# End states of a chunked mLSTM: VectorE copies the products' sums, GpSimd decays and adds the middle state

## The chip, the cores and the metric

The kernel runs on one core of a Trainium2 chip. The time is the device time of one execution in microseconds (us); the number given for a kernel is the median of its runs, 461.69 us for the kernel before (three runs). Five engines work side by side, each on its own queue in order: TensorE (PE in the profile, its weight loads PEld), VectorE (DVE), ScalarE (ACT), GpSimd (POOL) and SyncE (SP, which here only issues DMAs). They wait for one another through semaphores.

## The reference

An mLSTM cell with exponential gates runs over 4 batches x 8 heads, 768 steps, head size 40. Its output goes, token by token, through a two-layer network with a quick GELU (320 to 2048 to 320).

```python
for t in range(S):
    m_new = np.maximum(f_gate[:, :, t] + m, i_gate[:, :, t])
    f_stab = np.exp(f_gate[:, :, t] + m - m_new)
    i_stab = np.exp(i_gate[:, :, t] - m_new)
    C = f_stab * C + i_stab * outer(v_t, k_t)        # per head, 40 x 40
    n = f_stab * n + i_stab * k_t                    # per head, 40
    y_t = sigmoid(o_t) * (C @ q_t) / max(|n . q_t|, 1)
...
h = x @ w_in
g = h * (1.0 / (1.0 + np.exp(-1.702 * h)))
return g @ w_out
```

## The kernel before

**Windows.** The 768 steps are cut into six windows of 128 (w = 0 to 5). A window's attention is done in chunked form. For w of 1 and more, a window has two halves of 64 steps, and C and n together (40 x 41 per head) are a state that is known at three places: at the window's start (`state[w % 2]`), between the halves (`state_mid`) and at its end (`state[1 - w % 2]`). Sixteen pairs of heads lie in the free direction in two sets c = 0, 1 of eight pairs, so that one set of states is a 128 x 328 tile (8 x 41 columns).

**How a new state is made.** `carry` (L598) multiplies keys by gated values (`vw`, made by `scale` on GpSimd, L592) on TensorE. The sums for the middle state land in the PSUM tile `pair[0]`, those for the end state in `pair[1]`. The middle state is the start state times a decay plus the first sum: GpSimd multiplies (`decay` with x = 0, L583) ahead of the products, VectorE adds the sum (L616). The end state is the middle state times a second decay plus the second sum: VectorE multiplies (`decay` with x = 1, L583), and VectorE adds (L616). Both are done for c = 0, then for c = 1. Window 0 has one half and ScalarE copies its sums; window 5 needs no end state. So the two VectorE instructions per set run in windows 1 to 4.

**Who reads and who waits.** `values` (L515) of the same window multiplies queries by the start and the middle state. The end state is read first by `decay` of the next window. `pair` is also the PSUM tile of `scores` (L463) and of `values` (L507, L515): the scores of set c are written to `pair[c]`, which must have been read by VectorE before. VectorE multiplies the scores by the gate weights `wt` (L466). These weights are exponentials from ScalarE (L439, 16 per set) that GpSimd masks (`affine_select`, L443, two per set). After the second group of products, VectorE makes the outputs `u` (L521, L522, then L473 to L482). `u` and `vw` share a pool of two buffers (tag "u").

**Order.** There is no scheduler that reorders; every engine's queue has the order of the program text. The attention of window w + 1 is dealt out in pieces (`attention`, L926) between the blocks of the down projection of window w: after blocks of four f-tiles (`down`, L798) while w is 0, after the seven products of a Strassen-like scheme for each token half (`down_fast`, L852, with VectorE's additions L857 and `last_sums` L837) for w of 1 and more. Behind the attention pieces VectorE's queue holds, in window 1, four transposes of queries (L398) and the conversion of two pieces of the output weights (L256, L257, L259, L265), then the scores' product L466; in windows 2 to 4 two `last_sums` (L837), two additions (L857), then L466. GpSimd's queue holds `scale`, `decay`, four masks, and then, in window 1, a wait for the weights (`mark`, L596) and the weight sums (L811); in windows 2 to 4 nothing until the next up projection (`up_fast`, L729, L708, with GpSimd's L789).

Of the kernel before, what the change touches and what calls it, by code (L numbers as in the profile page):

```python
# [12 lines left out]
OP = mybir.AluOpType  # L13
# [13 lines left out]
def kernel(  # L27
# [14 lines left out]
    BH = B * H  # L42
# [5 lines left out]
    D1 = D + 1  # L48
# [6 lines left out]
    NJ = PH // 2  # L55
# [8 lines left out]
    op = ctx.enter_context(tc.tile_pool(name="op", bufs=2))  # L64
# [5 lines left out]
    V, A, G, T = nc.vector, nc.scalar, nc.gpsimd, nc.tensor  # L70
# [27 lines left out]
    def k_cols(w, t, h):  # L98

        return k_of(w)[t, h, 0:D] if w < 2 else k_st[t, h * D:h * D + D]  # L100
# [121 lines left out]
    state = [const.tile([128, BH // 2, D1], FP, name=f"state{i}") for i in range(2)]  # L222
    state_mid = const.tile([128, BH // 2, D1], FP, name="state_mid")

    m_at, ends = {0: m0}, {}
    cols, stacked, m_row, raw = {}, {}, {}, {}
    kT, qT, ys, xT, gs, o_ps, sums, vw, x_row = {}, {}, {}, {}, {}, {}, {}, {}, {}
# [105 lines left out]
    def slot(i, x):  # L333

        return slice((x ^ i) * HL, (x ^ i) * HL + HL)
# [239 lines left out]
            for n, k in ((0, slice(0, 2)), (1, slice(2, 3))):  # L575
                V.transpose(out=x[:, :, k], in_=x_square(c, n)[:, 4 * b:4 * b + 4].rearrange("p n (d c) -> p n c d", d=32))

    def decay(w, c, x, engine=G):

        js = slice(c * NJ, (c + 1) * NJ)  # L580
        d = cols[w][:, 3 * BH + x * BH // 2:3 * BH + (x + 1) * BH // 2][:, js]
        old, dst = ((state[w % 2], state_mid), (state_mid, state[1 - w % 2]))[x]
        engine.tensor_tensor(out=dst[:, js], in0=old[:, js], in1=d.unsqueeze(2).to_broadcast([128, NJ, D1]),  # L583
                             op=OP.mult)

    def scale(w, c, part=0, parts=1):
        n = PH // parts
# [10 lines left out]
    def carry(w, cs):  # L598
        n = 2 if 0 < w < NW - 1 else 1
        for c in cs:  # L600
            for j in range(NJ):
                for i in range(2):
                    for x in range(n):
                        t = slot(i, x) if w else slice(0, L)
                        T.matmul(pair[x][i * 64:i * 64 + D, c, j * D1:(j + 1) * D1],  # L605
                                 k_cols(w, t, c * PH + 2 * j + i), vw[w, c][t, 2 * j + i, :], start=True, stop=True)
        for x, dst in enumerate((state_mid, state[1 - w % 2])[:n]):
            for c in cs:
                js = slice(c * NJ, (c + 1) * NJ)
                new = pair[x][:, c, 0:NJ * D1].rearrange("r (j d) -> r j d", d=D1)  # L610
                if w == 0:
                    A.copy(out=state[1][:, js], in_=new)
                    continue
                if x:
                    decay(w, c, x, V)
                V.tensor_tensor(out=dst[:, js], in0=new, in1=dst[:, js], op=OP.add)  # L616


    def up(w, j, between):
# [305 lines left out]

    def attention(w):  # L926
        at = (0, 1, 3, 3, 5, 6, 8, 8, 9, 12, 14) if w == 1 else (0, 0, 1, 3, 1, 4, 5, 6, 6, 10, 11)
        calls = [[(columns, w), (scale, w, 0), (scale, w, 1), (decay, w, 0, 0), (decay, w, 1, 0)],
                 [(weights, w, 0)], [(weights, w, 1)], [(carry, w, (0, 1))], [(open_gates, w)],
                 [(scores, w, 0), (scores, w, 1)], [(values, w, 0)], [(seam_out, w, 0), (seam_in, w, 0)],  # L930
                 [(values, w, 1), (seam_out, w, 1), (seam_in, w, 1)], [(seam_turn, w, 0)], [(seam_turn, w, 1)]]
        side = {}
        for i, c in zip(at, calls):
            side.setdefault(i, []).extend(c)
        return side

    for w in range(NW):
        more = w + 1 < NW
        if w == 0:
            for j in range(NF // 2):  # L940
                if j % 2 == 0:
                    ahead, behind = converted[j // 2]
                    run([(convert, p) for p in ahead] + [(fetch, p) for p in fetched.get(j // 2, ())])
                    up(w, j, lambda: run([(columns_turn, 1) if p is None else (convert, p) for p in behind]))
                if j == 6:
                    load(1, "o")
                if j == 1:
                    wait_for(w_in_sb[:, 1, 512:1024])
                    scale(0, 1)
                    load(1, "v")  # L950
                if j < B and j % 2:
                    carry(0, (j // 2,))
                if j == 3:
                    masks()
                    gates(1)
                    columns_in(1)
                if j == 4:
                    spread(1)
                    load_squares(1, "q")
                if j >= B:  # L960
                    transposes(1, j - B)
        else:
# [23 lines left out]
            gelu_fast(w, NF // 2 - 1)  # L986
            hidden_sums(w, (2, 3), V)
        side = attention(w + 1) if more else {}
        if w == 0:

# [53 lines left out]
```

## Time and profile before

| | |
|---|---|
| runs | 461.58, 461.69, 464.37 us; median 461.69 |
| profiled execution | 463.3 us, of which the span of the trace is 461.6 us |
| TensorE busy | 452.8 us of the span, granted clock 1.00 |
| VectorE busy | 350.9 us |
| ScalarE busy | 186.0 us |
| GpSimd busy | 162.7 us, 155 instructions |
| VectorE, decay of the middle state (L583) | 8 instructions, 6.1 us |
| VectorE, adding the end sums (L616, `state`) | 8 instructions, 4.0 us |
| GpSimd, decay of the start state (L583) | 10 instructions, 9.3 us |
| GpSimd, masks (L443) | 20 instructions, 23.4 us |

A row of the timeline reads: start in us, length in us (of a run of equal instructions, from the first start to the last end), engine, line, operation, output and inputs, shapes, count, and in brackets the idle time of the engine before it with the event that ended it. A row of the waits reads: who waited for whom, us in total, times, longest. The chip's own wait instructions do not count as busy.

### The profile page before, as it was taken

Reading aid. Unit: us, or ns where it says so; the run is one execution under the profiler, and the core shown is the slowest. Engines: PE = TensorE matmul, PEld = TensorE weight load, DVE = VectorE, ACT = ScalarE, POOL = GpSimd, SP = SyncE. Lnnn points to the kernel's source line nnn. Section 1 sums busy time; section 2 is a strip of 40 time slices with the busy share of each in tenths; the row PEclk is TensorE's granted clock in tenths of the full one; section 3 lists DMA queues with packets and bytes.
Section 4 is the critical chain, followed back from the end, with each engine's and each line's share of the span. In section 5 each row is a group of like instructions: output and inputs, shape, how many; then the busy total and the mean of one; then the engine's idle time right before and its main releaser. Section 6 shows DMA issues by size and latency. Waiting matters only on the chain.

```text
span 461.6 us, 12375 instructions
## 1 busy us (share of the span) xinstructions
PE 452.8 (98%) x5071; PEld 386.5 (84%) x5071; DVE 350.9 (76%) x738; ACT 186.0 (40%) x433; POOL 162.7 (35%) x155
## 2 busy tenths in 40 slices
PE   8999999999999999999899999999999999999996
PEld 6777877775779999779899779999888999787996
DVE  6788998899988876889786888787788767554622
ACT  5686779100546600546700354900264810164100
POOL 5101318130677500266700167610157710146200
PEclk9999999999999999999999999999999999999999
DMA  8999999038969044959224979315989505000000
GB/s 165 186 289 195 251 234 221 5 67 186 179 138 122 3 102 115 193 79 174 36 61 109 195 117 165 50 37 122 176 130 156 76 18 141 28 1 1 1 28 30
DMA packets 135561, 52.87 MB, mean 115 GB/s; under 512 B 101984, under 2 KB 131632, under 8 KB 135504
## 3 DMA queue, kind: packets, MB, share of 16 engines
q1 hardware_dynamic: 127136, 50.27, 56.0%
q10 hardware_dynamic: 8048, 1.66, 1.8%
q8 instruction: 40, 0.66, 0.7%
q0 software_dynamic: 320, 0.15, 0.2%
q14 instruction: 17, 0.14, 0.1%
HBM read 44.52 MB, written 7.54 MB: 113 GB/s over the span
## 4 chain that ended last, share of the span: by engine, by line
PE 75%; DVE 11%; ACT 4%; SPq 4%; DMA 3%; issue 2%; DVEq 0%; ACTq 0%
PE p_out L852 30%; PE p_h L729 16%; PE p_a L729 6%; PE p_h L631 5%; PE p_h L708 4%; PE p_a L708 3%; SPq L120 2%; PE p_a L507 2%; DMA st_row<-f_run 2%; PE p_a L515 2%; PE p_a L463 2%; PE p_a L605 2%; ACT wt L439 2%; PE p_h L640 1%; PE p_a L390 1%
## 5 line engine op out<-in xcount | busy, mean ns | idle before, releaser
L789 POOL TENSOR_TENSOR g<-g,parts 128x512 f32<-128x512 f32 x30 | 38.2, 1274 | 184.7 <-ACT g L746 175.9
L768 ACT COPY parts<-p_h 128x256 f32<-128x256 f32 x40 | 14.9, 372 | 164.6 <-PE p_h L729 159.5
L852 PE MATMUL p_out<-w_out_sb,g 128*128 128x160 f32 x480 | 68.9, 300 | 0.0
L852 PEld LDWEIGHTS p_out<-w_out_sb,g 128*128 128x128 f32 x480 | 66.4, 190 | 0.5
L697 ACT ACTIVATE g<-g 128x512 f32<-128x512 f32 x80 | 47.7, 629 | 23.8 <-DVE g L783 18.8
L857 DVE TENSOR_TENSOR o_sb<-o_sb,p_out 128x160 f32<-128x160 f32 x70 | 21.4, 317 | 43.6 <-PE p_out L852 43.0
L852 PE MATMUL p_out<-t_sb,s 128*128 128x160 f32 x320 | 47.1, 300 | 0.0
L729 PE MATMUL p_h<-xT,w_in_sb 128*128 128x256 f32 x160 | 45.4, 386 | 0.0
L852 PEld LDWEIGHTS p_out<-t_sb,s 128*128 128x128 f32 x320 | 44.4, 190 | 0.2
L729 PE MATMUL p_h<-t_x,s_in 128*128 128x256 f32 x160 | 41.2, 380 | 0.2 <-DVE t_x L684 0.2
L439 ACT ACTIVATE wt<-wt,cols 128x64 f32<-128x64 f32 x160 | 38.8, 333 | 0.1
L729 PEld LDWEIGHTS p_h<-xT,w_in_sb 128*128 128x128 f32 x160 | 29.4, 190 | 9.8 <-issue 6.3
L798 PE MATMUL p_out<-w_out_sb,g 128*128 128x320 f32 x128 | 35.7, 436 | 0.0
L729 PEld LDWEIGHTS p_h<-t_x,s_in 128*128 128x128 f32 x160 | 30.2, 190 | 4.8 <-DVE t_x L684 0.6
L798 PEld LDWEIGHTS p_out<-w_out_sb,g 128*128 128x128 f32 x128 | 23.9, 190 | 9.6
L769 DVE TENSOR_TENSOR t_x<-p_h,parts 128x256 f32<-128x256 f32 x40 | 17.0, 425 | 16.8 <-ACT g L697 8.7
L631 PE MATMUL p_h<-xT,w_in_sb 128*128 128x256 f32 x128 | 29.6, 384 | 0.0
L631 PEld LDWEIGHTS p_h<-xT,w_in_sb 128*128 128x128 f32 x128 | 23.6, 190 | 5.3 <-issue 2.4
L820 POOL TENSOR_TENSOR g<-g 128x512 f32<-128x512 f32 x20 | 25.5, 1276 | 0.0
L443 POOL TENSOR_SCALAR_AFFINE_SELECT wt<-wt 64x1024 f32<-64x1024 f32 x20 | 23.4, 1170 | 5.4 <-ACT wt L439 4.7
L852 PE MATMUL p_out<-w_out_sb,s 128*128 128x160 f32 x160 | 23.8, 302 | 0.0
L852 PE MATMUL p_out<-t_sb,g 128*128 128x160 f32 x160 | 23.8, 302 | 0.0
(221 smaller groups left out, 892.4 us busy)
## 6 DMA issues: line engine op xcount, KB each, us to landing
q_sq<-in_q_dram SPq DMA_DIRECT2D x20, 320.0 KB, 10.2
wt<-m_row SPq DMA_DIRECT2D x20, 256.0 KB, 5.6
k_sq<-in_k_dram SPq DMA_DIRECT2D x16, 320.0 KB, 6.3
out_dram<-o_sb SPq DMA_DIRECT2D x24, 160.0 KB, 1.9
eo<-in_o_gate_dram SPq DMA_DIRECT2D x5, 640.0 KB, 8.5
bits<-in_moe_w_in_dram SPq DMA_DIRECT2D x6, 512.0 KB, 11.4
q_sq<-x_row SPq DMA_DIRECT2D x10, 256.0 KB, 2.9
v_st<-in_v_dram SPq DMA_DIRECT2D x14, 160.0 KB, 5.9
```

The source lines that it names most:

```text
L439: A.activation(out=x[:, h, :], in_=x[:, h, :], func=AF.Exp, scale=-1.0, bias=cols[w][:, c * PH + h:c * PH + h + 1])
L443: G.affine_select(out=r, in_=r, compare_op=OP.is_ge, fill=0.0, base=0, pattern=[[0, PH], [1, HL]], channel_multiplier=-1)
L631: T.matmul(ph[j][i][:, t], w_in_sb[:, c, f * 128:(f + 1) * 128], x[:, c, t], start=(first and c == 0 and n == 0), stop=(not first and c == ...
L697: A.activation(out=gs[w, j][:, i, :], in_=gs[w, j][:, i, :], func=AF.Gelu_apprx_sigmoid)
L708: T.matmul(row[:, t], w_in_x[r, j, :], xT[w][r, 2].rearrange("p b t -> p (b t)")[:, t], start=(start and h == 0), stop=(not start and h == ...
L729: T.matmul(out, a, x[n], start=start, stop=stop)
L769: V.tensor_tensor(out=u2, in0=p56[:, right], in1=y[:, left], op=OP.add)
L789: G.tensor_tensor(out=g0, in0=g0, in1=u, op=OP.add)
L798: T.matmul(po, gs[w, f // 2][:, f % 2, b * L:(b + 1) * L], w_out_sb[:, f, :], start=(f == 0), stop=(f == NF - 1))
L820: G.tensor_tensor(out=a10, in0=a00, in1=a10, op=OP.subtract)
L852: T.matmul(po, a(f), b[:, f, :], start=(f == 0), stop=(f == NH - 1))
L857: V.tensor_tensor(out=dst, in0=x, in1=po, op=OP.add)
```

## The change

VectorE no longer multiplies the middle state by its decay and no longer adds for the end state: in windows 1 to 4 it copies the second sum from PSUM into the end state's tile. Two new GpSimd instructions per set, at the end of `carry` and so behind the four masks in GpSimd's queue, multiply the middle state by its decay into the first 328 columns of the set's `vw` buffer, which the products have been read from by then, and add that to the end state's tile. `decay` keeps only its first form. The numbers of instructions per window: VectorE 6 before and 4 after, GpSimd 4 more.

```diff
-    def decay(w, c, x, engine=G):
+    def decay(w, c):
         js = slice(c * NJ, (c + 1) * NJ)
-        d = cols[w][:, 3 * BH + x * BH // 2:3 * BH + (x + 1) * BH // 2][:, js]
-        old, dst = ((state[w % 2], state_mid), (state_mid, state[1 - w % 2]))[x]
-        engine.tensor_tensor(out=dst[:, js], in0=old[:, js], in1=d.unsqueeze(2).to_broadcast([128, NJ, D1]),
-                             op=OP.mult)
+        d = cols[w][:, 3 * BH + c * NJ:3 * BH + (c + 1) * NJ]
+        G.tensor_tensor(out=state_mid[:, js], in0=state[w % 2][:, js], in1=d.unsqueeze(2).to_broadcast([128, NJ, D1]),
+                        op=OP.mult)
...
                 if w == 0:
                     A.copy(out=state[1][:, js], in_=new)
-                    continue
-                if x:
-                    decay(w, c, x, V)
-                V.tensor_tensor(out=dst[:, js], in0=new, in1=dst[:, js], op=OP.add)
+                elif x == 0:
+                    V.tensor_tensor(out=dst[:, js], in0=new, in1=dst[:, js], op=OP.add)
+                else:
+                    V.tensor_copy(out=dst[:, js], in_=new)
+        if n == 2:
+            for c in cs:
+                js, old = slice(c * NJ, (c + 1) * NJ), vw[w, c][:, 0:NJ, :]
+                d = cols[w][:, 3 * BH + BH // 2 + c * NJ:3 * BH + BH // 2 + (c + 1) * NJ]
+                G.tensor_tensor(out=old, in0=state_mid[:, js], in1=d.unsqueeze(2).to_broadcast([128, NJ, D1]), op=OP.mult)
+                G.tensor_tensor(out=state[1 - w % 2][:, js], in0=state[1 - w % 2][:, js], in1=old, op=OP.add)
...
-        calls = [[(columns, w), (scale, w, 0), (scale, w, 1), (decay, w, 0, 0), (decay, w, 1, 0)],
+        calls = [[(columns, w), (scale, w, 0), (scale, w, 1), (decay, w, 0), (decay, w, 1)],
```

## The prediction

> **What bounds the kernel now.** I read the page's busy table first, then TensorE's waits, then the timeline of each engine around the four places where the end state is made.
>
> ```profile
> PE 452.8 (98%) x5071; PEld 386.5 (84%) x5071; DVE 350.9 (76%) x738; ACT 186.0 (40%) x433; POOL 162.7 (35%) x155
> ```
>
> TensorE is busy for 452.8 of 461.6 us. Whatever VectorE saves is worth only what it takes out of TensorE's 8.8 us of idle time. So the question is which part of that idle time is a wait for VectorE behind the edited instructions. TensorE's waits (us in total, times, longest):
>
> ```profile
> PE p_h L729 <- DVE xT L576: 0.9, 1, 0.9
> PE p_a L507 <- DVE wt L466: 0.7, 3, 0.3
> PE p_a L463 <- DVE state L616: 0.6, 1, 0.6
> PE p_h L729 <- DVE t_x L684: 0.2, 1, 0.2
> ```
>
> These are 2.4 us, all on VectorE. The other named waits in that list belong to the start of the kernel, to a key load (0.6) and to issue. TensorE's timeline places them:
>
> ```profile
> 89.73 0.97 PE L507 MATMUL p_a<-v_st,wt 64*64 64x41 f32 x41 [0.26 <-DVE wt L466]
> 111.23 0.70 PE L729 MATMUL p_h<-xT,s_in 128*128 128x256 f32 x2 [0.87 <-DVE xT L576]
> 112.09 1.16 PE L729 MATMUL p_h<-t_x,s_in 128*128 128x256 f32 x4 [0.16 <-DVE t_x L684]
> ...
> 160.20 1.24 PE L507 MATMUL p_a<-v_st,wt 64*64 64x41 f32 x64 [0.20 <-DVE wt L466]
> ...
> 229.07 1.16 PE L463 MATMUL p_a<-qT,kT 40*64 40x64 f32 x64 [0.62 <-DVE state L616]
> ...
> 303.28 1.24 PE L507 MATMUL p_a<-v_st,wt 64*64 64x41 f32 x64 [0.20 <-DVE wt L466]
> ```
>
> So window 1 holds 1.29 us (0.26 + 0.87 + 0.16), window 2 0.20, window 3 0.62 and window 4 0.20. Now VectorE in window 1, and GpSimd beside it:
>
> ```profile
> 77.12 0.55 DVE L583 TENSOR_TENSOR state<-state_mid,cols 128x328 f32<-128x328 f32 x1
> 77.77 0.50 DVE L616 TENSOR_TENSOR state<-p_a,state 128x328 f32<-128x328 f32 x1
> 78.19 1.18 DVE L583 TENSOR_TENSOR state<-state_mid,cols 128x328 f32<-128x328 f32 x1
> 79.40 0.50 DVE L616 TENSOR_TENSOR state<-p_a,state 128x328 f32<-128x328 f32 x1
> 79.82 2.04 DVE L398 STREAM_TRANSPOSE qT<-q_sq 128x512 f32<-128x512 f32 x2
> ```
>
> ```profile
> 77.88 2.49 POOL L443 TENSOR_SCALAR_AFFINE_SELECT wt<-wt 64x1024 f32<-64x1024 f32 x2 [0.56 <-ACT wt L439]
> ```
>
> The multiply (L583) has two SBUF inputs and takes 0.49 at best; beside GpSimd's masks it takes 1.18 here and 1.24 in window 3. The addition (L616), with one input in PSUM, takes 0.49 to 0.50 in all eight cases, masks or not. The same holding-up is seen a little earlier:
>
> ```profile
> 70.19 1.39 DVE L257 TENSOR_SCALAR w_out_sb<-w_out_sb 128x512 uint32<-128x512 uint32 x1
> 71.62 1.66 DVE L259 SCALAR_TENSOR_TENSOR w_out_sb<-t_sb,w_out_sb 128x512 uint32<-128x512 uint32 x1
> 73.42 1.01 DVE L265 CUSTOM_DVE_ANT_0 w_out_sb<-t_sb,w_out_sb 128x1024 uint16<-128x1024 uint16 x1
> ```
>
> Beside GpSimd's `vw` multiplies (69.75 to 72.7) the conversion's 0.43 and 0.69 become 1.39 and 1.66: such an instruction waits for the end of the GpSimd instruction that it meets.
>
> **The change part by part.**
>
> *VectorE, removed: 8 multiplies*, 6.1 us in all (mean 761 ns). *Changed: 8 additions into copies from PSUM.* No row shows a 128x328 copy; the nearest are the copies from PSUM of 128x160 at 0.318 (an addition of that size: 0.317) and of 128x320 at 0.48. I take 0.49, equal to the addition, and nothing for the difference; the ends are 0.48 and 0.50. Being a PSUM read, I expect no hold-up by the masks.
>
> *GpSimd, added: 16 instructions*, 4 in each of windows 1 to 4. The multiply has a row of its own shape: L583 on GpSimd, 0.73 undisturbed, 0.95 on average, 1.18 at most. The addition has none; between 128x512 at 1.274 and 128x1280 at 2.904 the slope is 2.12 ns per element, and for 328 elements I work out an estimate of 0.88. A pair is 1.61, a window's four are 3.2, 13 us in all on an engine that is 35% busy. They lie behind the masks, so the masks are not later. Behind them in the queue: in window 1 the wait for the weights, which started at 90.16 and would now be reached at about 83.5; in windows 2 to 4 nothing before the next up projection some 20 us later. I cost them at nothing on GpSimd's own queue.
>
> *The new waits.* (a) GpSimd's additions wait for VectorE's copies, done before the last mask. (b) VectorE's L521 writes `u` into the buffer that GpSimd's first pair uses, and now waits for that pair. Window 2: masks end at 158.27, plus 1.61 gives 159.9; L521 starts at 162.54, or 162.3 if TensorE gains 0.2. Windows 3 and 4: about 231.6 against 234.1, and 303.0 against 305.4. Each has 2.4 us to spare; the second pair ends some 5 us before the second L521. Nothing is added.
>
> *The Trainium skill* (GPSIMD Engine Reference, "Engine selection") advises against exactly this move: two-input elementwise work belongs on VectorE, GpSimd being about twice as slow. The rows here say 0.73 against 0.49, 1.5 times; by the page's factor a pair would be an estimate of 2.0 us, still inside the 2.4 us, and the sum would not move.
>
> *Window 1.* VectorE's L398 starts at 79.82; without the two multiplies, and at the spacing of 0.41 between L616's, it starts at 77.12 + 2 x 0.41 = 77.95: 1.87 us earlier. But the four transposes (3.83 us) end then at 81.78, and the conversion's L256, L257 and L259 meet the new GpSimd instructions, which run from about 80.25 to 83.5. Before, GpSimd was idle from 80.38 on. L256 meets the first addition's last 0.1; L257 waits for the second multiply, about 0.6; L259 for the second addition, about 0.7. That takes 1.3 from 1.87, and about 0.6 is left. The ends: no hold-up, 1.87; all three held for a whole addition, 3 x 0.88 = 2.6, so 0.8 later than before. I take 0.6, as it follows the pattern of the three rows shown last. Behind that, VectorE is occupied without a gap from 92.09 to the token sums at 113 (L473 at 93.84 takes 2.39 instead of 0.17 until GpSimd's L811 ends, but L811 starts after L466 and moves with it), so TensorE gains what VectorE gains, up to its 1.29 us of waits: 0.6.
>
> *The rule behind this* is in the Trainium skill (SBUF — State Buffer, "Who interferes with whom"): GpSimd shares a pair of ports with VectorE as an exclusive lock for a whole instruction, against one-input VectorE work in a two-port mode and against two SBUF inputs, but not against at most one SBUF input. L616's steady 0.49 and L257's 1.39 agree. Without the lock window 1 would give 1.29 instead of 0.6, and the sum 2.3 instead of 1.6.
>
> *Window 2.* Additions at 153.35, copies from 154.17, `last_sums` (L837) from 155.0 instead of 156.28, then ahead of the masks that start at 155.86; L857 and L466 are ready by about 156.7 instead of 158.93. TensorE's L507 then follows its predecessor at 160.0: 0.20. *Window 4* is the same in every row: 0.20. *Window 3.* Copies end at 226.7, before TensorE has done the first set of scores (227.29 + 1.16), so the 0.62 goes; L837 is then held by masks until about 228.6, L466 starts at about 229.1 and ends its first half at 230.3, before L507 is due at 231.9. Next late there is nothing. 0.62.
>
> *Sum:* 0.6 + 0.20 + 0.62 + 0.20 = 1.6 us. Against the profiled execution's own 463.3 (span 461.6 and 1.7 around it) this gives 461.7. That execution is 1.6 above the median of the runs; from the median 461.69 the forecast is **460.1 us**.
>
> **The rivals.**
>
> *A: the hold-up eats window 1's gain, or more.* For it: the three rows above. Against it: only three instructions overlap. Windows 2 to 4 keep 1.0; window 1 gives 0 to -0.8: 460.7 to 461.5.
>
> *B: the gain does not last.* TensorE's carry products in window 3 waited 0.57 for a key load (223.57). If that chain of transfers did not move with TensorE, the 0.8 of windows 1 and 2 would reappear there: 460.9. Against it: the chain starts at VectorE's scan at 187.56, which follows TensorE.
>
> *C: slower, by VectorE's wait for the `u` buffer.* Place: L521 in windows 2 to 4. It begins to delay VectorE once a GpSimd pair takes 4.0 us instead of 1.61, TensorE (whose L507 at 164.77 has 0.5 to spare behind L522) from 4.5, and it makes the kernel slower than before from 5.0, since three windows then lose the 1.6 gained. At 6 us per pair: 3 x 1.5 - 1.6 = 2.9 slower, 464.6. For it: GpSimd's L583 stretches from 0.73 to 1.18 beside VectorE. Against it: VectorE runs only PSUM readers (L857, L466) there, and two at 1.3 make 2.6.
>
> **How the numbers follow.** The forecast has 0.58, its own range 459.4 (all 2.3 us of waits gone) to 461.0. A has 0.20, B 0.12, C 0.10. The range reaches down to 458.8 (the 2.3, and the key load's 0.57 gone too) and up to 462.3 (A's 461.5 and half of the 1.6 by which executions of the same kernel differ). A change of under 1%, 4.6 us, is about what a measurement of this kernel cannot tell from none. Faster by more would need twice the VectorE waits there are: 0.02. Slower by more needs C with pairs of over 6.5 us: 0.04. Within: 0.94.
>
> **What would show it.** Right: no L583 on VectorE, copies from PSUM at 0.49; L398 in window 1 some 1.9 us closer to L616; L257 and L259 there at about twice their 0.43 and 0.69; GpSimd pairs of about 1.6 us behind the masks; TensorE's waits for L616 gone, for L466 gone, for L576 at 0.3 to 0.7. Wrong: a wait of L521 for GpSimd; copies that stretch beside the masks; TensorE busy for the same share of an unchanged span.

## The result and the profile after

| | before | after |
|---|---|---|
| runs of this comparison | 8, 461.58 to 464.37 us | 8, 459.02 to 460.00 us |
| median | 462.17 us | **459.68 us** |
| ratio | | **0.9944**, 95% interval 0.9933 to 0.9954 |
| profiled execution, its span | 463.3, 461.6 us | 459.97, 458.3 us |

The kernel became faster by 0.56%, which is 2.6 us (2.1 to 3.1) of 462.2. The forecast was 460.1 us and a gain of 1.6. The time lies in the range, but the gain is an us larger than the terms of the sum.

The busy table after, the same line as at the head of the prediction:

```profile
PE 452.1 (99%) x5071; PEld 386.4 (84%) x5071; DVE 341.4 (75%) x730; ACT 185.5 (40%) x433; POOL 175.3 (38%) x171
```

VectorE lost 9.5 us and 8 instructions, GpSimd gained 12.6 us and 16. Of the 3.3 us by which the profiled span became shorter, 0.7 are busy time of TensorE (452.8 to 452.1) and the other 2.6 are idle time. TensorE's waits for VectorE behind the edited instructions were four groups with 2.4 us in all; after, two are left, with 0.6:

```profile
PE p_h L734 <- DVE xT L576: 0.4, 1, 0.4
PE p_h L734 <- DVE t_x L689: 0.2, 1, 0.2
```

The waits of the second products (L507) for `wt` and of the scores (L463) for the state are gone. The new instructions, from the views of their three lines (count: shortest/median/longest ns, first and last start, shapes):

```profile
L615 DVE COPY state<-p_a x8: 486/488/489, 77.7 to 294.8; 128x328 f32<-128x328 f32 x8
```

```profile
L620 POOL TENSOR_TENSOR vw<-state_mid,cols x8: 735/736/920, 80.9 to 300.2; 128x328 f32<-128x328 f32 x8
```

```profile
L621 POOL TENSOR_TENSOR state<-state,vw x8: 875/880/942, 81.8 to 301.0; 128x328 f32<-128x328 f32 x8
```

The copy takes 0.49 in all eight places, beside masks or not. Window 1 on VectorE before and after:

```profile
76.30 0.91 DVE L616 TENSOR_TENSOR state_mid<-p_a,state_mid 128x328 f32<-128x328 f32 x2 [1.88 <-PE p_a L605]
...
88.45 2.35 DVE L466 TENSOR_TENSOR wt<-p_a,wt 128x1024 f32<-128x1024 f32 x2
...
93.84 2.39 DVE L473 TENSOR_SCALAR den<-u 128x16 f32<-128x16 f32 x1
```

```profile
76.90 0.91 DVE L613 TENSOR_TENSOR state_mid<-p_a,state_mid 128x328 f32<-128x328 f32 x2 [1.89 <-POOL wt L443]
77.72 0.90 DVE L615 COPY state<-p_a 128x328 f32<-128x328 f32 x2
78.54 3.98 DVE L398 STREAM_TRANSPOSE qT<-q_sq 128x512 f32<-128x512 f32 x4
82.37 0.55 DVE L256 TENSOR_SCALAR w_out_sb<-w_out_sb 128x512 f32<-128x512 f32 x1
82.95 0.84 DVE L257 TENSOR_SCALAR w_out_sb<-w_out_sb 128x512 uint32<-128x512 uint32 x1
83.82 1.25 DVE L259 SCALAR_TENSOR_TENSOR w_out_sb<-bits,w_out_sb 128x512 uint32<-128x512 uint32 x1
...
88.17 2.35 DVE L466 TENSOR_TENSOR wt<-p_a,wt 128x1024 f32<-128x1024 f32 x2
...
93.63 1.90 DVE L473 TENSOR_SCALAR den<-u 128x16 f32<-128x16 f32 x1
```

On GpSimd, again before and after:

```profile
90.16 0.19 POOL L596 COPY mark<-wt 128x1 f32<-128x1 f32 x1 [9.79 <-DVE wt L466]
...
93.30 2.90 POOL L811 TENSOR_TENSOR t_sb<-w_out_sb,t_sb 128x1280 f32<-128x1280 f32 x1
```

```profile
80.94 0.74 POOL L620 TENSOR_TENSOR vw<-state_mid,cols 128x328 f32<-128x328 f32 x1
81.75 0.88 POOL L621 TENSOR_TENSOR state<-state,vw 128x328 f32<-128x328 f32 x1
82.59 0.92 POOL L620 TENSOR_TENSOR vw<-state_mid,cols 128x328 f32<-128x328 f32 x1
83.58 0.94 POOL L621 TENSOR_TENSOR state<-state,vw 128x328 f32<-128x328 f32 x1
89.46 0.19 POOL L595 COPY mark<-wt 128x1 f32<-128x1 f32 x1 [4.93 <-DVE wt L466]
...
92.59 2.91 POOL L816 TENSOR_TENSOR t_sb<-w_out_sb,t_sb 128x1280 f32<-128x1280 f32 x1
```

From the first state addition to the first transpose (L398) it is 1.64 us; before, it was 79.82 - 76.30 = 3.52. That is 1.88 gained. Two instructions give some of it back: L257 (0.84 for 0.43) and L259 (1.25 for 0.69) meet the GpSimd pairs. L466, the scores' product, then starts 11.27 us after the first state addition; before, it was 88.45 - 76.30 = 12.15. So at L466 VectorE keeps 0.88 of 1.88.

Further on it gains 0.42 more. The first L473 of the window is held until GpSimd has done its two weight sums (L811 before, L816 after): it ends 0.03 us behind the second of them in both kernels. These sums follow `mark`, GpSimd's wait for the weights of L466, and `mark` starts 1.71 us after L466 starts before, but 1.29 after. From the first state addition to the end of L473 it is 19.93 us before and 18.63 after: 1.30 gained, and from there to the transposes for which TensorE waits (L576) VectorE has no gap.

In windows 2 to 4 nothing on VectorE waits for GpSimd. Window 2, VectorE and then TensorE:

```profile
161.44 0.84 DVE L521 TENSOR_TENSOR u<-p_a,cols 128x656 f32<-128x656 f32 x1 [1.79 <-PE p_a L515]
```

```profile
156.85 2.44 PE L857 MATMUL p_out<-t_sb,g 128*128 128x160 f32 x16
159.22 1.14 PE L507 MATMUL p_a<-v_st,wt 64*64 64x41 f32 x64
```

L521, which writes the buffer that GpSimd's first pair uses, waits for TensorE (L515) as before, and L507 follows its predecessor without a wait; before, it stood 0.20 behind `wt`.

**Where the time went, by stage.** For the three profiled executions of the kernel before and the two of the kernel after, from the start of the first state product of one window (line `carry`, L605 before, L604 after, of window 1 at 74 to 75 us) to that of the next, read from TensorE's timeline. The column "window 1" thus runs from the products of window 1's state to those of window 2's; the last column runs to the end of the span. The rows below `after_again` are of the runs described further down:

| us | to window 1's products | window 1 | 2 | 3 | 4 | rest |
|---|---|---|---|---|---|---|
| before | 74.37 | 77.41 | 70.93 | 72.15 | 70.98 | 95.75 |
| before_again | 74.22 | 77.35 | 70.98 | 70.98 | 71.35 | 95.75 |
| before_third | 74.71 | 77.29 | 70.94 | 71.08 | 70.98 | 95.76 |
| after | 74.96 | 76.11 | 70.47 | 70.47 | 70.50 | 95.75 |
| after_again | 74.45 | 76.12 | 70.46 | 70.47 | 70.50 | 95.75 |
| w1_only | 75.03 | 76.28 | 70.97 | 70.99 | 71.21 | 95.75 |
| w234_only | 74.21 | 78.66 | 70.47 | 70.47 | 70.50 | 95.76 |
| no_gpsimd | 74.21 | 75.41 | 70.46 | 70.47 | 70.50 | 95.75 |
| no_gpsimd_w1 | 75.17 | 75.45 | 70.47 | 70.48 | 70.64 | 95.76 |
| long_pair | 74.25 | 77.95 | 71.37 | 71.38 | 71.41 | 95.76 |
| deferred | 74.32 | 75.87 | 71.13 | 71.08 | 71.05 | 95.76 |
| hybrid | 74.20 | 75.98 | 70.46 | 70.47 | 70.64 | 95.75 |

The first column is the same code in every kernel and varies by 1.0 us, which the change did not cause. The change acts in the next four: 1.2 to 1.3 us in window 1, as much as the 1.30 by which VectorE's L473 ends sooner, about 0.5 in windows 2, 3 and 4, and more where an execution of the kernel before was late (72.15, 71.35).

### The profile page after: what moved, and what is told of

It is laid out like the page before. It is cut to its first block, busy times and chain, and to the rows that moved or that the text cites. A ratio compares the mean times of both kernels' runs of the same rounds, so it can differ in the third digit from the quotient of the medians.

```text
span 458.3 us, 12396 instructions
## 1 busy us (share of the span) xinstructions
PE 452.1 (99%) x5071; PEld 386.4 (84%) x5071; DVE 341.4 (75%) x730; ACT 185.5 (40%) x433; POOL 175.3 (38%) x171
## 4 chain that ended last, share of the span: by engine, by line
PE 93%; DVE 5%; issue 1%; POOL 1%; ACT 0%; POOLq 0%; DVEq 0%
PE p_out L857 34%; PE p_h L734 19%; PE p_a L734 8%; PE p_h L636 6%; PE p_out L803 4%; PE p_h L713 4%; PE p_a L713 4%; PE p_a L463 2%; PE p_a L507 2%; PE p_a L515 2%; PE p_a L604 2%; PE p_h L645 2%; PE p_a L390 1%; PE p_s L452 1%; DVE xT L576 1%
## 5 line engine op out<-in xcount | busy, mean ns | idle before, releaser
L591 POOL TENSOR_TENSOR vw<-v_st,cols 128x656 f32<-128x656 f32 (+1 forms) x13 | 16.7, 1299 | 19.0 <-issue 10.3
```

## The experiments

The theory was the prediction's own: TensorE gains the time for which it stood behind VectorE's end state, all of it in windows 2 to 4, and in window 1 what the GpSimd pairs leave by holding up VectorE's conversion. What had to be told apart was which windows the gain comes from, why it is larger than the waits add up to, whether the hold-up is real, and what rival C (VectorE waits for the `u` buffer) would cost. Kernels that ran together: before_again, w1_only, w234_only and no_gpsimd; then deferred, no_gpsimd_w1, long_pair and before_third; then hybrid and after_again.

### The kernel before again: what is chance

No edit. Two more profiled executions of the kernel before; the first with 12 timed runs.

> The kernel before, unchanged, profiled once more and timed against itself. Theory 1 (the gain is VectorE's lateness in windows 1 to 4 and nothing else): TensorE waits again for VectorE at L507 in windows 1, 2 and 4 (0.26, 0.20, 0.20 us) and for L576 in window 1 (0.87), while the 0.57 us wait for the key load in window 3 and the 0.62 us wait at L463 that followed it were that one execution's: in a second profile the key load is in time, window 3 looks like windows 2 and 4 (0.20 at L507), and the span is about 460.5 instead of 461.6. Theory 2 (the key load and the L463 wait belong to every execution, and the change removes both): both waits stand again at 0.4 to 0.7 us and the span is 461.2 to 461.8. Ratio to itself 1.000 in either case, within 0.001.

> The kernel before, profiled a third time. Told apart: which waits belong to every execution. Expected in each: 0.25 us idle at L507 in windows 1 and 2 (and 70.9 to 71.0 us for window 2), 0.87 at L576 in window 1; the key load's wait in window 3 absent, as in two of three; the wait at L463 behind L616 in window 3 or 4 at most once, 0.2 to 0.4; the carry products of window 1 interrupted before their last two for 0.2 to 0.3, if that belongs to this program and not to an execution.

before_again took 462.98 us against 462.69, ratio 1.0006 (0.9993 to 1.0019); before_third 462.46 in its one run. In the first profile TensorE had waited 0.57 in window 3 for a key load; in neither of the two new ones is there such a wait. The 0.62 of window 3 (L463 behind the state) is not fixed either. In before_again it is smaller and in window 4; its TensorE timeline has:

```profile
160.03 1.24 PE L507 MATMUL p_a<-v_st,wt 64*64 64x41 f32 x64 [0.25 <-DVE wt L466]
...
231.00 1.24 PE L507 MATMUL p_a<-v_st,wt 64*64 64x41 f32 x64 [0.24 <-DVE wt L466]
...
298.71 1.16 PE L463 MATMUL p_a<-qT,kT 40*64 40x64 f32 x64 [0.27 <-DVE state L616]
```

In before_third all three windows wait for `wt`; window 3 only in the weight loads' row, and there its second set of scores waits for the state too, where in the other executions it follows the first set without a gap:

```profile
227.87 1.02 PEld L463 LDWEIGHTS p_a<-qT,kT 40*64 40x64 f32 x64 [0.17 <-DVE state L616]
...
231.48 1.12 PEld L507 LDWEIGHTS p_a<-v_st,wt 64*64 64x64 f32 x64 [0.32 <-DVE wt L466]
```

So the late key load was a matter of one execution. There the state products of window 3 took 0.83 us longer than in the kernel after (2.20 to the next down products, for 1.37), and the scores with the wait of 0.62 took 0.85 longer (2.87, for 2.02); the two make the 1.68 by which 72.15 lies above 70.47. But each of windows 2 to 4 of the kernel before is 0.46 us or more longer than after, whichever of the two waits it shows.

### The change in window 1 alone, and in windows 2 to 4 alone

w1_only, against the kernel after; the other windows keep VectorE's multiplication and addition:

```diff
-                else:
+                elif w == 1:
                     V.tensor_copy(out=dst[:, js], in_=new)
-        if n == 2:
+                else:
+                    d = cols[w][:, 3 * BH + BH // 2 + c * NJ:3 * BH + BH // 2 + (c + 1) * NJ]
+                    V.tensor_tensor(out=dst[:, js], in0=state_mid[:, js], in1=d.unsqueeze(2).to_broadcast([128, NJ, D1]),
+                                    op=OP.mult)
+                    V.tensor_tensor(out=dst[:, js], in0=new, in1=dst[:, js], op=OP.add)
+        if n == 2 and w == 1:
```

w234_only is the same with `w > 1` in both places.

> The new end states in window 1 only; windows 2 to 4 as before. Theory 1: TensorE's 0.26 at L507 in window 1 goes, its 0.87 at the first up product behind L576 shrinks to about 0.44, so 0.7 us faster than before (0.9985). Theory 2 says the same 0.7 for this part, but leaves the window 3 waits of about 1.2 us in. Rival (nothing of window 1 lasts): 1.000.

> The new end states in windows 2 to 4 only; window 1 as before. Theory 1: 0.20 to 0.27 us in each of three windows, 0.7 us in all (0.9985), and window 1's waits stand as before (0.26, 0.87, 0.16). Theory 2: 0.7 plus the key load's 0.57 and the L463 wait's 0.4 beyond that, 1.7 us (0.9963).

w1_only: 461.50 us, ratio 0.9974 (0.9962 to 0.9986), which is 1.2 us (0.6 to 1.8) of 462.7. w234_only: 460.80, 0.9959 (0.9945 to 0.9973), 1.9 us (1.2 to 2.5). The two add up to 3.1, beside 2.6 (2.1 to 3.1) for the whole change and 3.1 (2.4 to 3.9) for after_again below. In the table each kernel has the short stages just where it has the edit: 76.28 in window 1 for w1_only, 70.47 to 70.50 in windows 2 to 4 for w234_only. The gain of windows 2 to 4, 1.9 us, is larger than the sum of their waits (0.20, 0.62 and 0.20), and the two parts do not need each other. In w234_only's profiled execution, its longest (461.77), window 1 took 78.66, more than in any execution of the kernel before; VectorE had waited 1.53 us for a transfer ahead of it (L360). The other seven runs took 460.17 to 461.11.

**Why 0.20 is worth 0.46.** Inside window 2, from the first scores (L463) to the first set's second products (L507) it is 4.67 us before and 4.40 after, and from there to the other set's L507 it is 4.57 and 4.37: 0.27 and 0.20 less, for a wait that TensorE's row shows as 0.20. The weight loads' row of the kernel before:

```profile
160.20 1.12 PEld L507 LDWEIGHTS p_a<-v_st,wt 64*64 64x64 f32 x64 [0.44 <-DVE wt L466]
...
162.40 1.66 PEld L852 LDWEIGHTS p_out<-w_out_sb,s 128*128 128x128 f32 x12
```

and after:

```profile
159.22 1.02 PEld L507 LDWEIGHTS p_a<-v_st,wt 64*64 64x64 f32 x64 [0.17 <-issue]
...
161.22 2.20 PEld L857 LDWEIGHTS p_out<-w_out_sb,s 128*128 128x128 f32 x16
```

The loads stop for 0.17 in front of this block even where nothing is late. A wait that ends at 0.44 has cost 0.27 of that, and that is the first part. The second part lies behind the wait: from the block's start to the next down products it is 2.20 us before and 2.00 after. All of it is in L507's own block: from its first load to L515's first it is 1.13 us before (160.20 to 161.33) and 0.92 after (159.22 to 160.14), and from there to the next down products 1.07 and 1.08. So the price has two terms, and TensorE's row of waits gives neither. The three executions of the kernel before bear this out: in windows 2 to 5 eight L507 blocks have a wait for `wt` in the loads' row (0.32 to 0.49), and each takes 2.20 us to the next down products; the other sixteen have 0.17 and take 2.00 or 2.01. Why the block itself runs slower after a wait is not shown by any run. It can do so without one: in window 4 of no_gpsimd_w1 and of hybrid the second L507 block waits for nothing and still takes 0.12 longer to the next down products (2.12, for 2.00 in the kernel after), which is most of the 70.64 against 70.50 in the table.

### Without the GpSimd instructions: the hold-up

```diff
-        if n == 2:
+        if False:
```

and for no_gpsimd_w1 `if n == 2 and w > 1:`.

> The changed kernel without GpSimd's 16 new instructions: the decayed middle state is left out of the end state, VectorE's copies stay. If GpSimd's new instructions cost only by holding up L257 and L259 in window 1 (port theory): L257 and L259 are back at 0.43 and 0.69, L466 starts about 1 us earlier, TensorE's remaining 0.44 wait behind L576 goes to 0 and 0.17 behind the token sums stays or goes, so 0.4 to 0.6 us faster than the changed kernel, 2.9 to 3.1 us faster than before (0.9936). If they cost nothing: equal to the changed kernel (0.9944) and the 0.44 stays. If they cost more, at places not seen: over 1 us faster than the changed kernel.

> The changed kernel without GpSimd's new instructions in window 1 alone (its end state lacks the decayed middle state there); in windows 2 to 4 GpSimd works as in the changed kernel. Port theory (GpSimd's work costs in window 1 only): window 1 takes 75.4 us, windows 2 to 4 take 70.47, 70.47 and 70.51 as with no new GpSimd work at all; ratio to before 0.992. Rival (it costs in windows 2 to 4 too): these stay longer than without the work by 0.1 or more each; ratio 0.993 or above.

no_gpsimd: 458.83 us, ratio 0.9919 (0.9901 to 0.9936). no_gpsimd_w1: 459.43, 0.9929 (0.9914 to 0.9944). In the table the pairs of window 1 cost 0.66 to 0.70 us (76.11 against 75.45 and 75.41), those of windows 2 to 4 nothing (70.46 to 70.50 with and without them; the one 70.64 is the block named above). VectorE in window 1 of no_gpsimd:

```profile
81.56 0.42 DVE L256 TENSOR_SCALAR w_out_sb<-w_out_sb 128x512 f32<-128x512 f32 x1
82.02 0.43 DVE L257 TENSOR_SCALAR w_out_sb<-w_out_sb 128x512 uint32<-128x512 uint32 x1
82.48 0.69 DVE L259 SCALAR_TENSOR_TENSOR w_out_sb<-bits,w_out_sb 128x512 uint32<-128x512 uint32 x1
...
86.27 2.35 DVE L466 TENSOR_TENSOR wt<-p_a,wt 128x1024 f32<-128x1024 f32 x2
```

With the pairs away, L257 and L259 are back at 0.43 and 0.69, and TensorE's wait for `xT` is gone. So it is the pairs that stretch them. L466 starts 10.13 us after the first state addition (76.14), 1.14 sooner than in the kernel after. But `mark` starts 1.71 after L466 again, not 1.29, so that L473 ends only 0.72 sooner, and that is the stage's 0.70. In all four executions with the pairs in window 1 `mark` starts 1.28 or 1.29 after L466 (after, after_again, w1_only, long_pair), in all eight without them there 1.70 to 1.72. So the pairs cost 1.14 and give 0.42 back. Why GpSimd then starts sooner, no run shows.

### A long first pair: rival C made real

In windows 2 to 4 the first multiplication is done five times:

```diff
+                for _ in range(4 if w > 1 and c == 0 else 0):
+                    G.tensor_tensor(out=old, in0=state_mid[:, js], in1=d.unsqueeze(2).to_broadcast([128, NJ, D1]), op=OP.mult)
                 G.tensor_tensor(out=old, in0=state_mid[:, js], in1=d.unsqueeze(2).to_broadcast([128, NJ, D1]), op=OP.mult)
```

> The changed kernel with the first set's multiply done five times instead of once in windows 2 to 4, so that a GpSimd pair takes 4.9 us instead of 1.6 (the result is the same). It tests the prediction's rival C: VectorE's L521 should start when the pair ends, 1.0 us later than now. By the prediction's price (TensorE late from 4.5 us, one for one) 0.4 per window, 1.2 us slower than the changed kernel. If a wait of TensorE costs 0.3 us beyond its idle time, because its weight loads stop too (theory from windows 2 and 3 before: 0.25 idle, 0.5 lost), 0.55 + 0.3 per window, 2.5 us slower than the changed kernel, ratio to before about 1.000. If the buffer is not waited for, no difference to the changed kernel.

long_pair: 462.61 us against 462.21, ratio 1.0002 (0.9989 to 1.0015). VectorE and TensorE in window 2:

```profile
163.69 0.84 DVE L521 TENSOR_TENSOR u<-p_a,cols 128x656 f32<-128x656 f32 x1 [2.91 <-POOL state L623]
```

```profile
165.51 1.20 PE L507 MATMUL p_a<-v_st,wt 64*64 64x41 f32 x61 [0.71 <-POOL state L623]
```

```profile
165.48 1.11 PEld L507 LDWEIGHTS p_a<-v_st,wt 64*64 64x64 f32 x61 [0.93 <-POOL state L623]
```

The wait that rival C named now exists, in the place that it named. The first set's GpSimd instructions run from 158.71 to 163.66, 4.95 us, and each of the three windows becomes 0.90 longer (71.37 to 71.41 against 70.47 to 70.50). The weight loads' row gives 0.93 - 0.17 = 0.76 of that, the slower block behind it about 0.1 (2.12 us from L507's start to the next down products, 2.00 in the kernel after). The kernel is back at the time of before. Its window 1, 77.95, is not of this edit: the profiled execution is the longest of this kernel's runs, VectorE's transposes (L398) waited 1.85 us there for the load of the queries, and TensorE then 1.5 for `wt`.

### The end state behind the next gates: deferred, and a hybrid

deferred moves GpSimd's four instructions away from the conversion: they are issued after the first up-projection group of the window, and multiply in place in `state_mid`. hybrid does so for window 1 only and keeps the change elsewhere.

```diff
-        if n == 2:
-            for c in cs:
...
+    def end_state(w):
+
+        for c in range(2):
+            js = slice(c * NJ, (c + 1) * NJ)
+            d = cols[w][:, 3 * BH + BH // 2 + c * NJ:3 * BH + BH // 2 + (c + 1) * NJ]
+            G.tensor_tensor(out=state_mid[:, js], in0=state_mid[:, js], in1=d.unsqueeze(2).to_broadcast([128, NJ, D1]), op=OP.mult)
+            G.tensor_tensor(out=state[1 - w % 2][:, js], in0=state[1 - w % 2][:, js], in1=state_mid[:, js], op=OP.add)
...
+                if more and j == 0:
+                    end_state(w)
```

> GpSimd's end states moved out of the attention: multiplied in place in the middle state's tile and added behind GpSimd's first instruction of the next up projection, where VectorE reads PSUM only and GpSimd waited before. VectorE copies as in the changed kernel. Port theory: window 1 (first carry product to first carry product of window 2) takes 75.4 us as without GpSimd's work, against 76.1 in the changed kernel and 77.4 before; windows 2 to 4 stay at 70.5; 0.7 us faster than the changed kernel, ratio to before 0.992. Rival (GpSimd's work costs wherever it stands, for instance by delaying its additions in the up projection for ScalarE's GELU): the up projection grows and the ratio is 0.9944 or more.

> A version meant to beat both: the end states of windows 2 to 4 as in the changed kernel (behind the masks, where they cost nothing), that of window 1 in place in the middle state's tile behind GpSimd's first instruction of window 1's up projection, where GpSimd waited for VectorE before. By the stage times so far: window 1 takes 75.3 to 75.5 us (as without GpSimd's work) and windows 2 to 4 70.47 to 70.51, so 0.7 us faster than the changed kernel run beside it, ratio to before about 0.9925. If the up projection of window 1 grows as those of windows 2 to 4 did in the deferred version (by 0.6), no gain over the changed kernel.

> The changed kernel once more, beside the version that is meant to beat it. Ratio to before 0.9944 as measured, within 0.001; the stages again at 70.47, 70.47 and 70.51 us in windows 2 to 4, window 1 at 76.1 or longer where an input of its conversions lands later.

deferred: 461.40 us, ratio 0.9976 (0.9966 to 0.9986). hybrid: 459.79, 0.9941 (0.9922 to 0.9960); beside it after_again: 459.49, 0.9932 (0.9915 to 0.9949). Moving the instructions did take them off the conversion: in hybrid L466 of window 1 starts 10.14 us after the first state addition (86.28 - 76.14), in the kernel after 11.27. But the new place costs too: the expectation had overlooked the instructions of the gates there. GpSimd and VectorE of deferred at the new place in window 2:

```profile
186.31 0.85 POOL L622 TENSOR_TENSOR state_mid<-state_mid,cols 128x328 f32<-128x328 f32 x1
187.24 0.88 POOL L623 TENSOR_TENSOR state<-state,state_mid 128x328 f32<-128x328 f32 x1
188.07 0.85 POOL L622 TENSOR_TENSOR state_mid<-state_mid,cols 128x328 f32<-128x328 f32 x1
189.00 0.94 POOL L623 TENSOR_TENSOR state<-state,state_mid 128x328 f32<-128x328 f32 x1
```

```profile
186.66 0.64 DVE L290 TENSOR_TENSOR st<-fi,f_run 32x128 f32<-32x128 f32 x1
187.34 1.05 DVE L296 TENSOR_TENSOR_SCAN m_run<-one,m_end,st 32x128 f32<-32x128 f32 x1
188.42 0.51 DVE L311 TENSOR_TENSOR m_end<-f_run,m_run 32x1 f32<-32x1 f32 x1
...
189.21 0.78 DVE L317 TENSOR_SCALAR st<-st,m_run 32x64 f32<-32x64 f32 x1
```

and the same VectorE instructions in the kernel after:

```profile
187.48 0.28 DVE L290 TENSOR_TENSOR st<-fi,f_run 32x128 f32<-32x128 f32 x1
187.80 0.47 DVE L296 TENSOR_TENSOR_SCAN m_run<-one,m_end,st 32x128 f32<-32x128 f32 x1
188.30 0.15 DVE L311 TENSOR_TENSOR m_end<-f_run,m_run 32x1 f32<-32x1 f32 x1
...
188.72 0.25 DVE L317 TENSOR_SCALAR st<-st,m_run 32x64 f32<-32x64 f32 x1
```

The gates' small instructions take 0.64 for 0.28, 1.05 for 0.47, 0.51 for 0.15 and 0.78 for 0.25: 1.83 us more together. The additions of the up projection stand behind them in VectorE's queue and start 4.77 us after L290 for 2.90, and TensorE's up projection becomes 0.54 to 0.66 us longer in windows 2 to 4 (32.42 to 32.50 for 31.84 to 31.88), where the old place had cost nothing. In hybrid the same happens in window 1 alone, whose up projection takes 33.23 for 32.67 in no_gpsimd: that eats most of the 0.70, and the gain there is the 0.13 us of the table, less than the intervals can show. No version was found that beats the kernel after.

## Why the prediction was right, and where it was mis-sized

**Right: what was removed and added.** VectorE's copy 0.49 (forecast 0.49, untouched by masks); L398 earlier by 1.88 (forecast 1.87); GpSimd's addition 0.88 (the estimate from the slope), its multiplication 0.74, a pair 1.69 from start to end (forecast 1.61); GpSimd's pairs behind the masks; no wait of L521.

**Right: the hold-up in window 1 (rival A's mechanism, the forecast's size).** The forecast took 1.3 of 1.87 away and left 0.6 at L466; 1.0 was taken and 0.88 left. L257 lost 0.41 (said: 0.6), L259 0.56 (said: 0.7). no_gpsimd_w1 shows that the pairs do it. The rule of the Trainium skill (SBUF — State Buffer, "Who interferes with whom") held in both directions: the copy with its input in PSUM took 486 to 489 ns in all eight places, and L257 and L259 were at 0.84 and 1.25 with the pairs, at 0.43 and 0.69 without.

**Mis-sized: window 1's term, 0.6.** It measured 1.2 to 1.3 in the stages (77.29 to 77.41, then 76.11 and 76.12) and 1.2 (0.6 to 1.8) in w1_only. That TensorE gains what VectorE gains was right; VectorE's gain was taken too small in two places. At L466 it is 0.88. Behind it the prediction put L473 at nothing, since "L811 starts after L466 and moves with it". GpSimd's weight sums start 0.42 sooner after L466 than before, and L473, which ends with them, takes 1.90 instead of 2.39. 0.88 and 0.42 are the 1.30 of the stage. TensorE's own delays ahead of that do not count, since it waits for VectorE behind them: its state products and what lies between them and the scores took 8.04 to 8.50 us in the three executions before, and the stage was the same within 0.12.

**Failed: the step that priced windows 2 and 4 at 0.20 each by TensorE's row.** The prediction counted the idle time shown in front of L507. The stages lost 0.46 and 0.48: the weight loads lost 0.27 in front of the block, and the block itself ran 0.2 slower. With 0.5 for each of windows 2 to 4, and window 1 at its 1.2, the sum is 2.7; the runs say 2.6.

**Near in size, wrong in place: window 3's 0.62.** That wait was one execution's, and there it cost 0.85. Other executions of the kernel before have a wait for `wt` there, or a smaller wait for the state in window 4. The stage of window 3 gained 0.51 and 0.61 against these.

**The rivals.** A did not decide: no window was slower. B (the key load) did not come: neither execution of the kernel after shows that wait, and only the first of the three of the kernel before does. C has the mechanism that the prediction gave, and it needs a pair about three times as long. Its price was too low by the same fault as windows 2 and 4: at 4.95 us the prediction allows 0.45 a window, and 0.90 was measured, so the gain is used up at about 4.9 us rather than 5.0. That the two lie so close is luck: the gain and the price were both taken too low. The Trainium skill (GPSIMD Engine Reference, "Engine selection") speaks against moving two-input elementwise work to GpSimd; here GpSimd took 1.5 and 1.8 times VectorE's 0.49 for it, and the kernel was faster, because most of that time lay where TensorE did not wait for it.

**The base.** The forecast subtracted from a median of three runs, 461.69; larger samples gave 462.2 to 462.9. That is why the time came out within 0.4 us although the gain was 0.9 to 1.0 larger; that part of the agreement is luck. The prediction also took a change of under 1% to be one that cannot be told from none; with eight runs of each kernel the interval was 0.1% to either side, and 0.56% stood clear of it.

**Open.** What sometimes interrupts the state products of window 1 for 0.3 to 0.5 us, with no releaser in the profile; why a block of small matmuls runs slower behind a wait; and why GpSimd starts `mark` sooner when its pairs ran before it. Other places for window 1's pairs than the two tried were not tried.

## What to carry to other kernels

Here it paid to move work to an engine that was 35% busy from the one on which TensorE waited, even though each instruction took 1.5 to 1.8 times as long there. It cost TensorE's stages nothing where nothing waited for it (windows 2 to 4), and 0.7 us where it met VectorE's conversion (window 1). Price a wait in front of a block of many small matmuls by the length of the stage around it, with and without the wait where two executions allow it, and not by the matmul row's idle time. Before pricing a single wait, look at a second execution: the waits of windows 3 and 4 were not in the same place there. And when an instruction is held until another engine is done, follow that engine too: it need not move by as much as the instruction ahead of it.

## What the runs showed of the hardware that was not expected

- In front of a block of 64 matmuls of 41 columns, a wait of 0.20 in the matmul row cost 0.46 of the stage, and one of 0.71 cost 0.90. In the weight loads' row the same waits are 0.44 and 0.93, of which 0.17 is there without any wait; the remainder is the block itself, which ran 0.2 (eight blocks of eight in the kernel before) and 0.1 slower after the wait (and 0.12 slower without one in window 4 of no_gpsimd_w1 and hybrid).
- Beside GpSimd's two-input instructions even VectorE's tiny ones are held: 32x1 elements took 0.51 for 0.15, and a scan of 32x128 1.05 for 0.47.
- On GpSimd, for the same 128x328 elements, the multiplication by a broadcast column took 0.736 us and the addition of two full tiles 0.880.
- GpSimd's `mark`, released by the same VectorE instruction, started 1.28 or 1.29 us after that instruction's start where GpSimd had run its pairs shortly before (idle for 4.93 us), and 1.70 to 1.72 where it had not (idle for 7.87 to 10.94 us). Whether the idle time is the reason, no run shows.
